# Attention and max-out layer on one core: operand splits moved in the time table, q and k loaded by halves, one ordered section instead of two, the last weight part on VectorE

## The chip, the cores and the metric

The kernel runs on one core of one Trainium2 chip. The metric is device time in microseconds of that core; the time before is the median of three runs. A profile of one further execution shows what each engine did. The engines are named as the profile names them: PE (TensorE matmul), PEld (TensorE weight load), DVE (VectorE), ACT (ScalarE), POOL (GpSimd) and SP (SyncE, which here only issues DMAs).

## The reference

Attention in chunks of 64 positions, then a layer that takes the largest of three products and multiplies it by an output matrix. Everything is float32.

```python
scores = scale * np.matmul(q_c, k_c.transpose(0, 1, 2, 4, 3))      # chunks of 64, head_dim 64
scores = scores - np.max(scores, axis=-1, keepdims=True)
attn = np.exp(scores)
attn = attn / (np.sum(attn, axis=-1, keepdims=True) + 1e-09)
out = np.matmul(attn, v_c)
...
x = np.ascontiguousarray(attn_out.transpose(0, 2, 1, 3)).reshape(B * S, H * D)   # 4608 x 512
h = np.maximum(np.maximum(x @ w1, x @ w2), x @ w3)                               # 512 -> 768
return (h @ w_out).astype(np.float32)                                            # 768 -> 512
```

## The kernel before

**Tiles and groups.** The 4608 tokens are 36 tiles of 128 tokens (two chunks with eight heads each). Four tiles make a group; there are nine groups, 0 to 8. A group's hidden products `x @ w` (lines 148 to 150, written into `pm`) need the `x` of all its four tiles, then its output products follow (same lines, from `hh`, `hl`, `woh`, `wol`). So that float32 accuracy comes out of fast products, every operand is split into a high part, rounded by ScalarE (`xh`, `hh`, `wh`, `woh`), and a low part, which is the operand minus its high part (`xl`, `hl`, `wl`, `wol`); each product is then three matmuls: low weight by high data (L148), high weight by low data (L149), high by high (L150).

**Attention of a tile** (`attention`, tiles 8 to 35). One DMA loads q and k of the tile together into `r` (1 MB). ScalarE casts q into `qs` (L270) and k in two halves into `kk` (L292); GpSimd subtracts to get the low parts (L274 for `qs`, L296 twice for `kk`). PE forms the scores `s` of chunk 0 and of chunk 1 (four matmuls each, L252); `s` is one PSUM buffer, so the second product waits until ScalarE (L258) and VectorE (L263) have taken the first out into `e`. VectorE takes the maximum, GpSimd subtracts it (L318), ScalarE exponentiates (L323), VectorE sums, GpSimd normalizes (L165), VectorE transposes into `et` (L338), ScalarE and VectorE split that into `ah` (L343, L347). `ah` goes through DRAM (`there`) and comes back as `aa` (L352, L359). `v` is loaded as `rv` and split into `vs` in the same way. PE forms `x` of both chunks from `aa` and `vs` (L252), ScalarE and VectorE take it out as `xs` (L258, L263), and `xh` (ScalarE, L373) and `xl` (VectorE, L378) are the tile's part of the next-but-one group's operand.

**What sets the order.** Each engine executes in the order in which the program hands it work. Two ordered sections are written: the first follows the list `FIRST` (weights, tiles 0 to 7, hidden layer of group 0); the second walks through the products of the remaining groups at a step of 0.6815 and takes every other operation from a heap when its due time has come. The due times are written in `attention` relative to the tile's first score product: `r` at -13.0, `qs` at -5.7 and -4.4, `kk` at -4.5, -3.9 and -2.0, -0.7, `xh` at 30.3, and so on. Between the two sections a scheduler has placed the first instructions of the second among the last of the first: the load of tile 8's `r` stands among the weight loads on SP, and its `qs` and `kk` splits stand ahead of the last weight parts on ScalarE and GpSimd. The token `Y65p` at the end of `FIRST` puts the low part of the last piece of the output weights (`wol`, L143) on GpSimd.

**A group's start.** The first L149 of a group's hidden products reads `xl` and waits for the `xl` of the group's last tile. That tile's `xh` and `xl` fall into the same stretch as the `qs` split of a later tile, on ScalarE one right behind the other.

Of the kernel before, what the change touches and what calls it, by code (L numbers as in the profile page):

```python
# [9 lines left out]
F32 = mybir.dt.float32  # L10
# [10 lines left out]
P = 128  # L21
# [6 lines left out]
PLAIN = 8  # L28
# [17 lines left out]
B51 F22f h30f C51 hh2f D51 X51 Y42 H51 W60 h31f B52 Y51 A52 hl2f C52 D52 h32f X52 B60 W61 A60 F30f C60 xh6 D60 H52  # L46
xl6 h40f at7 X60 Y52 W62 A61 F31f H60 Y60 V7 F32f C61 hh3f D61 h41f B61 hl3f A62 X61 B62 C62 W63 H61 D62 F40f h42f
X62 F41f W64 H62 Y61 Y62 A63 h50f F42f C63 hh4f D63 A64 hl4f B63 C64 h51f B64 X63 xh7 D64 W65 F50f X64 H63 H64 h52f
F51f Y63 Y64 B65 A65 F52f C65 hh5f D65 hl5f X65 xl7 H65 Y65p
"""  # L50


# [1 line left out]
def chunk_attn_maxout_kernel(  # L54
# [12 lines left out]
    nc = tc.nc  # L67
# [3 lines left out]
    att = ctx.enter_context(tc.tile_pool(name="att", bufs=1))  # L71
# [161 lines left out]

    halves_of = [slice(0, 64), slice(64, 128)]

    def attention(t, x_of, col):

# [1 line left out]
        st = {}  # L241
        ops = []

        def due(at, pe=0.0):
            return lambda fn: ops.append((at, pe, fn))
# [19 lines left out]
        def stack(at, low_at, name, tag, src):  # L265

            @due(at)
            def _():
                st[name] = att.tile([P, 2, 4, P], F32R, name=name, tag=tag, bufs=1)
                nc.scalar.copy(out=st[name], in_=src())  # L270

            @due(low_at)
            def _():
                nc.gpsimd.tensor_tensor(out=st[name][64:], in0=src()[64:], in1=st[name][64:].bitcast(F32), op=ALU.subtract)  # L274

        @due(-13.0)
        def _():
            st["r"] = att.tile([P, 2, 2, 4, P], F32, name="r", tag="raw", bufs=1)
            nc.sync.dma_start(out=st["r"], in_=qk2[t - PLAIN])

        @due(8.5)
        def _():
            st["rv"] = att.tile([P, 2, 4, P], F32, name="rv", tag="rv", bufs=1)
            nc.sync.dma_start(out=st["rv"], in_=v2[t - PLAIN])

        stack(-5.7, -4.4, "qs", "qs", lambda: st["r"][:, 0])
        for c in range(2):
            @due(-4.5 + 0.6 * c)
            def _(c=c):
                if c == 0:  # L290
                    st["kk"] = att.tile([P, 2, 4, 2, P], F32R, name="kk", tag="kk", bufs=1)
                nc.scalar.copy(out=st["kk"][:, c, :, 0, :], in_=st["r"][:, 1, c])  # L292

            @due(-2.0 + 1.3 * c)
            def _(c=c):
                nc.gpsimd.tensor_tensor(out=st["kk"][:, c, :, 1, :], in0=st["r"][:, 1, c],  # L296
                                        in1=st["kk"][:, c, :, 0, :].bitcast(F32), op=ALU.subtract)

        def e_of(c):
            if "e" not in st:  # L300
                st["e"] = ep.tile([P, 4, 2, 64], F32, name="e")
            return st["e"][:, :, c, :]

        for c in range(2):
            products((0.0, 3.3)[c], (1.0, 4.3)[c], ps_s, "s", lambda g, c=c: st["qs"][:, c, g, :],
                     lambda g, c=c: st["kk"][:, c, g].rearrange("p a x -> p (a x)"), lambda c=c: e_of(c))
# [57 lines left out]
        def x_cols(c):  # L364
            if "xs" not in st:
                st["xs"] = xs_p.tile([P, 4, P], F32, name="xs")
            return st["xs"][:, :, c * 64:(c + 1) * 64]

        for c in range(2):
            products((24.0, 27.7)[c], (25.0, 29.3)[c], ps_x, "x", lambda g, c=c: st["vs"][:, c, g, :],  # L370
                     lambda g, c=c: st["aa"][:, :, :, 2 * g + c].rearrange("p n a x -> p a n x"), lambda c=c: x_cols(c))
# [79 lines left out]
    starts = [sum(GROUPS[:i]) for i in range(len(GROUPS))]  # L451
    halves = {}
    def x_tiles(i):
        if i not in halves:
            halves[i] = [xp.tile([P, CT, 512], F32R, name=n) for n in ("xh", "xl")]
        return halves[i]
# [19 lines left out]
    def idle_products(n):  # L476
        ps = ps_m.tile([P, 512], F32, name="pm")
        for _ in range(n):
            nc.tensor.matmul(out=ps, lhsT=idle[:, :P], rhs=idle[:, :512], start=True, stop=True)

    nc.vector.memset(idle, 0.0)
    ET = mybir.EngineType
    with tc.manual_schedule(engines={ET.PE, ET.DVE, ET.Activation, ET.Pool, ET.SP}):
        for name in FIRST.split():
            if name[0] == "i":
                idle_products(int(name[1:]))
            elif name[-1] == "p":
                ops[name[:-1]](nc.gpsimd)
            elif name[:3] == "nrm":
                ops[name](nc.vector)  # L490
            else:
                ops[name]()
# [4 lines left out]
    due = []  # L497

    def plan(at, pe, fn):
        heapq.heappush(due, (at, len(order), pe, fn))  # L500
        order.append(fn)

    order = []
    for i in range(2, len(GROUPS)):
        for tt in range(4):
            first = (i - 1) * total - 33.0 + (tt - 3) * (15.4 if i == 2 else total / 4)
            for at, pe, fn in attention(starts[i] + tt, lambda i=i: x_tiles(i), tt * P):
                plan(first + at, pe, fn)

    parts = [g0["project"](0, 1), g0["project"](2), g0["project"](3)]  # L510
# [3 lines left out]
        parts += [g["project"](0, 1), g["project"](2), g["project"](3)]  # L514
    now = -4 * JT * STEP - 2 * BLOCK
    with tc.manual_schedule(engines={ET.PE, ET.DVE, ET.Activation, ET.Pool, ET.SP}):
        for part in parts:
            for after in part:
                now += STEP
                for at, fn in after:  # L520
                    plan(now + at, 0.0, fn)
                while due and due[0][0] <= now:
                    _, _, pe, fn = heapq.heappop(due)
                    fn()
                    now += pe
        while due:
            heapq.heappop(due)[3]()
# [42 lines left out]
```

## Time and profile before

| | before |
|---|---|
| median of 3 runs | 711.55 us (711.12 to 712.19) |
| the profiled execution: time, span | 709.78 us, 707.7 us |
| PE busy | 694.7 us (98%), 3401 instructions |
| DVE, ACT, POOL busy | 404.1, 356.3, 297.7 us (57%, 50%, 42%) |
| granted TensorE clock | 1.0 over the span |
| DMA | 121.20 MB, 171 GB/s in the mean |

A busy share near 100% says that PE has few idle moments, not that every one of its steps is as short as it can be. So the table of who waited for whom is read for PE, and then the timeline around each of these waits. In a row of the timeline the first number is the start in microseconds from the start of the span, the second the length (of all instructions of the row together, where x is more than 1), then follow engine, line, operation and tiles, and in brackets the idle time of the engine before it with what ended it.

### The profile page before, as it was taken

How to read it: one execution, taken by the hardware profiler on the slowest of the kernel's cores; microseconds unless marked ns; L12 is line 12 of the kernel's file. 1: busy time of each engine (PE TensorE's matmuls, PEld its weight loads, DVE VectorE, ACT ScalarE, POOL GpSimd, SP SyncE). 2: the span in 40 equal slices, each digit the busy share in tenths (PEclk: the TensorE clock that was granted, in tenths of full speed). 3: DMA queues.
4: the chain of work that ended last, by engine and by line, in shares of the span. 5: the costliest groups of instructions: out<-in, count | busy, mean ns of one | idle time of the engine just before them, and what ended most of it. 6: DMA issues, size and time to landing. Idle time of an engine off the chain costs nothing.

```text
span 707.7 us, 9475 instructions
## 1 busy us (share of the span) xinstructions
PE 694.7 (98%) x3401; PEld 575.6 (81%) x3402; DVE 404.1 (57%) x721; ACT 356.3 (50%) x663; POOL 297.7 (42%) x191
## 2 busy tenths in 40 slices
PE   8999999999999999999999999999999999999998
PEld 4998878778888888888888888888888888888886
DVE  6988863587466654665466546664666456622220
ACT  5666653556555554554555555555555545531111
POOL 1422033565545455555555555545445545510000
PEclk9999999999999999999999999999999999999999
DMA  9975414566755566555855385547555755440001
GB/s 359 370 282 179 144 38 171 169 193 196 223 176 178 164 210 192 179 179 145 271 178 157 113 265 157 167 149 241 163 167 178 223 170 173 119 134 15 1 1 59
DMA packets 38318, 121.20 MB, mean 171 GB/s; under 512 B 3456, under 2 KB 3456, under 8 KB 34688
## 3 DMA queue, kind: packets, MB, share of 16 engines
q1 hardware_dynamic: 38272, 120.60, 52.6%
q8 instruction: 27, 0.44, 0.3%
q14 instruction: 19, 0.16, 0.1%
HBM read 96.47 MB, written 24.12 MB: 170 GB/s over the span
## 4 chain that ended last, share of the span: by engine, by line
PE 72%; issue 7%; ACT 6%; POOL 6%; DVE 5%; DMA 4%; SPq 0%; POOLq 0%; ACTq 0%; DVEq 0%
PE pm L148 20%; PE pm L150 20%; PE pm L149 20%; PE s L252 4%; POOL kk L296 4%; PE x L252 4%; ACT qs L270 3%; DVE xs L263 2%; PE x L219 2%; DMA buf<-in_wout 2%; ACT xh L373 1%; PE s L186 1%; POOL qs L274 1%; DMA r<-in_qk 1%; DMA xl<-in_w 1%
## 5 line engine op out<-in xcount | busy, mean ns | idle before, releaser
L148 PE MATMUL pm<-xh,wl 128*128 128x512 f32 (+1 forms) x660 | 256.8, 389 | 0.0
L150 PE MATMUL pm<-xh,wh 128*128 128x512 f32 (+1 forms) x660 | 255.2, 387 | 0.0
L149 PE MATMUL pm<-xl,wh 128*128 128x512 f32 (+1 forms) x660 | 254.7, 386 | 0.0
L150 PEld LDWEIGHTS pm<-xh,wh 128*128 128x128 f32 x660 | 124.0, 188 | 26.4
L149 PEld LDWEIGHTS pm<-xl,wh 128*128 128x128 f32 x660 | 124.2, 188 | 22.3
L148 PEld LDWEIGHTS pm<-xh,wl 128*128 128x128 f32 x660 | 124.1, 188 | 22.0
L263 DVE TENSOR_TENSOR e<-s,e 64x256 f32<-64x256 f32 x112 | 47.3, 422 | 145.4 <-ACT e L258 144.6
L274 POOL TENSOR_TENSOR qs<-r,qs 64x1024 fp32r<-64x1024 f32 x28 | 70.5, 2517 | 110.0 <-ACT qs L270 83.5
L412 DVE TENSOR_TENSOR m<-pm,m 128x512 f32<-128x512 f32 (+1 forms) x110 | 74.7, 679 | 40.4 <-PE pm L150 38.5
L258 ACT COPY e<-s 64x256 f32<-64x256 f32 x112 | 41.2, 367 | 106.1 <-PE s L252 105.3
L149 PE MATMUL pm<-wol,hh 128*128 128x512 f32 x216 | 84.3, 390 | 0.8 <-POOL wol L143 0.8
L148 PE MATMUL pm<-woh,hl 128*128 128x512 f32 x216 | 84.7, 392 | 0.0
L150 PE MATMUL pm<-woh,hh 128*128 128x512 f32 x216 | 84.3, 390 | 0.0
L296 POOL TENSOR_TENSOR kk<-r,kk 128x512 fp32r<-128x512 f32 x56 | 79.3, 1436 | 2.2
L274 POOL TENSOR_TENSOR vs<-rv,vs 64x1024 fp32r<-64x1024 f32 x28 | 67.2, 2400 | 13.7 <-ACT vs L270 6.0
L258 ACT COPY xs<-x 64x256 f32<-64x256 f32 x112 | 41.1, 367 | 52.9 <-PE x L252 52.0
L421 DVE TENSOR_TENSOR hl<-m,hh 128x512 fp32r<-128x512 f32 (+1 forms) x54 | 56.0, 1036 | 19.1 <-ACT hh L418 18.6
L318 POOL TENSOR_TENSOR e<-e,mx 128x512 f32<-128x512 f32 x28 | 29.2, 1044 | 87.9 <-DVE mx L314 87.9
L165 POOL TENSOR_TENSOR e<-e,sm 128x512 f32<-128x512 f32 x31 | 32.4, 1044 | 73.0 <-DVE sm L162 72.6
L263 DVE TENSOR_TENSOR xs<-x,xs 64x256 f32<-64x256 f32 x112 | 47.3, 422 | 26.1 <-ACT xs L258 24.6
L418 ACT CAST hh<-m 128x512 fp32r<-128x512 f32 (+1 forms) x55 | 33.7, 613 | 48.5 <-DVE m L412 47.6
L410 ACT COPY m<-pm 128x512 f32<-128x512 f32 (+1 forms) x55 | 31.9, 580 | 37.0 <-DVE hl L421 21.2
(66 smaller groups left out, 785.3 us busy)
## 6 DMA issues: line engine op xcount, KB each, us to landing
r<-in_qk SPq DMA_DIRECT2D x28, 1024.0 KB, 6.0
aa<-there SPq DMA_DIRECT2D x56, 512.0 KB, 5.7
rv<-in_v SPq DMA_DIRECT2D x28, 512.0 KB, 5.4
there<-ah SPq DMA_DIRECT2D x28, 512.0 KB, 2.6
out_x<-ao SPq DMA_DIRECT2D x36, 256.0 KB, 2.2
buf<-in_qk SPq DMA_DIRECT2D x8, 768.0 KB, 8.4
buf<-in_w SPq DMA_DIRECT2D x10, 512.0 KB, 3.8
buf<-in_vb SPq DMA_DIRECT2D x8, 512.0 KB, 6.8
```

What stands on the lines that cost most here:

```text
L148: nc.tensor.matmul(out=o, lhsT=al, rhs=bh, start=first, stop=False)
L149: nc.tensor.matmul(out=o, lhsT=ah, rhs=bl, start=False, stop=False)
L150: nc.tensor.matmul(out=o, lhsT=ah, rhs=bh, start=False, stop=last)
L165: eng.tensor_tensor(out=e, in0=e, in1=sm.unsqueeze(2).broadcast_to([P, 8, 64]), op=ALU.mult)
L252: nc.tensor.matmul(out=o[:, g].rearrange("p a h x -> p (a h x)"), lhsT=lhs(g), rhs=rhs(g), start=True, stop=True)
L258: nc.scalar.copy(out=out()[rows], in_=st[name][rows, :, 0, h, :])
L263: nc.vector.tensor_tensor(out=out()[rows], in0=st[name][rows, :, 1, h, :], in1=out()[rows], op=ALU.add)
L274: nc.gpsimd.tensor_tensor(out=st[name][64:], in0=src()[64:], in1=st[name][64:].bitcast(F32), op=ALU.subtract)
L296: nc.gpsimd.tensor_tensor(out=st["kk"][:, c, :, 1, :], in0=st["r"][:, 1, c], in1=st["kk"][:, c, :, 0, :].bitcast(F32), op=ALU.subtract)
L412: nc.vector.tensor_tensor(out=banks[j][:, :n], in0=ps[j, w][:, :n], in1=banks[j][:, :n], op=ALU.max)
L418: nc.scalar.copy(out=hh[j][:, lo:hi], in_=banks[j][:, :hi - lo])
L421: eng.tensor_tensor(out=hl[j][:, lo:hi], in0=banks[j][:, :hi - lo], in1=hh[j][:, lo:hi].bitcast(F32), op=ALU.subtract)
```

## The change

Four edits. The `qs` and `kk` splits of a tile fall due earlier by `lead` (0.8 for the tiles of group 2, 1.5 for those of later groups). `r` is one buffer for all tiles, loaded by two DMAs of 0.5 MB, q due at -16.6 and k at -14.6. The list `FIRST` is worked off inside the same ordered section as the time table. The last token is `Y65`, which puts that low part on VectorE.

```diff
-F51f Y63 Y64 B65 A65 F52f C65 hh5f D65 hl5f X65 xl7 H65 Y65p
+F51f Y63 Y64 B65 A65 F52f C65 hh5f D65 hl5f X65 xl7 H65 Y65
...
-    def attention(t, x_of, col):
+    loaded = {}
+
+    def attention(t, x_of, col, lead):
...
-        @due(-13.0)
-        def _():
-            st["r"] = att.tile([P, 2, 2, 4, P], F32, name="r", tag="raw", bufs=1)
-            nc.sync.dma_start(out=st["r"], in_=qk2[t - PLAIN])
+        for half, at in enumerate((-16.6, -14.6)):
+            @due(at)
+            def _(half=half):
+                if "r" not in loaded:
+                    loaded["r"] = att.tile([P, 2, 2, 4, P], F32, name="r", tag="raw", bufs=1)
+                st["r"] = loaded["r"]
+                nc.sync.dma_start(out=st["r"][:, half], in_=qk2[t - PLAIN][:, half])
...
-        stack(-5.7, -4.4, "qs", "qs", lambda: st["r"][:, 0])
+        stack(-5.7 - lead, -4.4 - lead, "qs", "qs", lambda: st["r"][:, 0])
         for c in range(2):
-            @due(-4.5 + 0.6 * c)
+            @due(-4.5 + 0.6 * c - lead)
...
-            @due(-2.0 + 1.3 * c)
+            @due(-2.0 + 1.3 * c - lead)
...
-    with tc.manual_schedule(engines={ET.PE, ET.DVE, ET.Activation, ET.Pool, ET.SP}):
+    def first_group():
         for name in FIRST.split():
...
-            for at, pe, fn in attention(starts[i] + tt, lambda i=i: x_tiles(i), tt * P):
+            for at, pe, fn in attention(starts[i] + tt, lambda i=i: x_tiles(i), tt * P, 0.8 if i == 2 else 1.5):
...
     with tc.manual_schedule(engines={ET.PE, ET.DVE, ET.Activation, ET.Pool, ET.SP}):
+        first_group()
         for part in parts:
```

In the changed file the lines from `attention` on lie 3 to 9 lines further down (L270 becomes L273, L373 L380, L343 L350, L433 L440). PE executes the same instructions in the same order as before.

**ScalarE around the start of group 2.** `ao` is an output of group 1, `ah` and `xh` belong to older tiles, `qs` and `kk` are the splits of a later tile. Before:

```order
L433 COPY ao<-pm 128x512
L343 CAST ah<-et 128x2x256
L373 CAST xh<-xs 128x4x128
L270 CAST qs<-r 128x1024
L292 CAST kk<-r 128x4x128 x2
L433 COPY ao<-pm 128x512
```

Now:

```order
L440 COPY ao<-pm 128x512
L350 CAST ah<-et 128x2x256
L273 CAST qs<-r 128x1024
L380 CAST xh<-xs 128x4x128
L299 CAST kk<-r 128x4x128 x2
L440 COPY ao<-pm 128x512
```

`qs` has moved ahead of `xh`. The same exchange stands at every later tile that still has a `qs` split behind it, inside the groups as well as at the starts of groups 2 to 7; GpSimd and VectorE keep their order there.

**ScalarE at the end of the first group.** `woh` are the high parts of the output weights (the last one is piece 65), `buf` and `ao` prepare that piece, `qs` and `kk` belong to tile 8. Before:

```order
L140 CAST woh<-ao 128x512 x2
L270 CAST qs<-r 128x1024
L292 CAST kk<-r 128x4x128 x2
L124 ACTIVATE buf<-buf 128x512
L120 ACTIVATE ao<-buf 128x512
L418 CAST hh<-m 128x512
L140 CAST woh<-ao 128x512
```

Now:

```order
L140 CAST woh<-ao 128x512 x2
L124 ACTIVATE buf<-buf 128x512
L120 ACTIVATE ao<-buf 128x512
L425 CAST hh<-m 128x512
L140 CAST woh<-ao 128x512
L273 CAST qs<-r 128x1024
L299 CAST kk<-r 128x4x128 x2
```

Tile 8's splits now stand behind the last weight piece, on ScalarE and on GpSimd; `wol` of that piece has left GpSimd and stands on VectorE behind the last `xl` of the first group.

**SP around the first tiles of the time table.** `there` and `aa` carry `ah` through DRAM, `rv` is v. Before, tiles 8 and 9:

```order
L284 DMA rv<-in_v 128x1024
L352 DMA there<-ah 128x1024
L359 DMA aa<-there 64x4x512 x2
L279 DMA r<-in_qk 128x2048
```

Now:

```order
L291 DMA rv<-in_v 128x1024
L359 DMA there<-ah 128x1024
L286 DMA r<-in_qk 128x1024
L366 DMA aa<-there 64x4x512 x2
L286 DMA r<-in_qk 128x1024
```

The q half stands between `there` and `aa` at these two tiles; from tile 10 on both halves stand behind `aa`, where the whole load stood. The first load of `r` has moved from among the weight loads to behind the last of them.

## Rows read from the trace of the kernel before

**Rows 1.** Who waited for whom, PE alone: total us, times, longest

```profile
PE s L252 <- POOL kk L296: 4.5, 19, 1.1
```

**Rows 2.** Timeline, PE, around the two score products of a later tile

```profile
213.38 0.39 PE L150 MATMUL pm<-xh,wh 128*128 128x512 f32 x1
213.94 0.74 PE L252 MATMUL s<-kk,qs 128*128 128x256 f32 x4 [0.18 <-POOL kk L296]
214.52 0.40 PE L148 MATMUL pm<-xh,wl 128*128 128x512 f32 x1
...
217.02 0.39 PE L150 MATMUL pm<-xh,wh 128*128 128x512 f32 x1
217.25 0.64 PE L252 MATMUL s<-kk,qs 128*128 128x256 f32 x4
217.72 0.40 PE L148 MATMUL pm<-xh,wl 128*128 128x512 f32 x1
```

**Rows 3.** Timeline, other engines, ahead of that score product

```profile
207.03 0.62 ACT L343 CAST ah<-et 128x512 fp32r<-128x512 f32 x1 [1.38 <-DVE et L338]
207.92 0.62 ACT L373 CAST xh<-xs 128x512 fp32r<-128x512 f32 x1 [0.27 <-DVE xs L263]
208.45 1.04 ACT L270 CAST qs<-r 128x1024 fp32r<-128x1024 f32 x1
...
209.25 0.68 DVE L378 TENSOR_TENSOR xl<-xs,xh 128x512 fp32r<-128x512 f32 x1
...
209.62 2.57 POOL L274 TENSOR_TENSOR qs<-r,qs 64x1024 fp32r<-64x1024 f32 x1 [3.37 <-ACT qs L270]
...
209.85 0.68 DVE L412 TENSOR_TENSOR m<-pm,m 128x512 f32<-128x512 f32 x1
...
211.22 1.53 DVE L421 TENSOR_TENSOR hl<-m,hh 128x512 fp32r<-128x512 f32 x1 [0.69 <-ACT hh L418]
...
212.84 0.59 ACT L410 COPY m<-pm 128x512 f32<-128x512 f32 x1 [0.70 <-DVE hl L421]
```

**Rows 4.** Timeline, VectorE and GpSimd, where their subtractions overlap

```profile
153.81 2.40 POOL L274 TENSOR_TENSOR qs<-r,qs 64x1024 fp32r<-64x1024 f32 x1 [1.17 <-ACT qs L270]
154.75 2.01 DVE L347 TENSOR_TENSOR ah<-et,ah 128x512 fp32r<-128x512 f32 x1 [0.35 <-ACT ah L343]
156.29 3.32 POOL L296 TENSOR_TENSOR kk<-r,kk 128x512 fp32r<-128x512 f32 x2
156.69 1.77 DVE L421 TENSOR_TENSOR hl<-m,hh 128x512 fp32r<-128x512 f32 x1
```

**Rows 5.** Timeline around the start of a group's hidden products

```profile
262.91 0.62 ACT L343 CAST ah<-et 128x512 fp32r<-128x512 f32 x1 [0.21 <-DVE et L338]
...
264.45 0.69 DVE L378 TENSOR_TENSOR xl<-xs,xh 128x512 fp32r<-128x512 f32 x1
...
266.18 0.39 PE L149 MATMUL pm<-xl,wh 128*128 128x512 f32 x1
```

**Rows 6.** Copies of scores (the page's costliest groups), and a restart of PE

```profile
L258 ACT COPY e<-s 64x256 f32<-64x256 f32 x112 | 41.2, 367 | 106.1 <-PE s L252 105.3
...
160.62 0.86 DVE L263 TENSOR_TENSOR e<-s,e 64x256 f32<-64x256 f32 x2
161.63 0.71 PE L252 MATMUL s<-kk,qs 128*128 128x256 f32 x4 [0.20 <-ACT vs L270]
```

**Rows 7.** Timeline, the last piece of the output weights

```profile
101.67 0.62 ACT L140 CAST woh<-ao 128x512 fp32r<-128x512 f32 x1 [4.19 <-DVE ao L137]
103.69 0.50 PE L149 MATMUL pm<-wol,hh 128*128 128x512 f32 x1 [0.84 <-POOL wol L143]
```

**Rows 8.** Timeline, PE, two waits at tiles 10 and 9

```profile
141.21 0.74 PE L252 MATMUL s<-kk,qs 128*128 128x256 f32 x4 [1.12 <-POOL kk L296]
150.33 0.73 PE L252 MATMUL x<-aa,vs 128*128 128x256 f32 x4 [0.36 <-DMA aa<-there]
```

**Rows 9.** DMA issues (the page): KB each, median us to landing

```profile
r<-in_qk SPq DMA_DIRECT2D x28, 1024.0 KB, 6.0
```

## The prediction

> **What bounds the kernel now.** I read the table of who waited for whom for PE first, then the timeline around each wait. PE is busy 98% of the span, so only its waits and what could become one matter. The table has one repeated wait: the score products wait for `kk` from GpSimd, 19 times, 4.5 us idle in all [rows 1]. One of these is 1.12 us [rows 8]; the other 18 are 0.19 us each. I count 17 of them from 213.94 on, at three of four tiles, and one at tile 11.
>
> What one costs is more than its idle time. From the matmul before the scores to the matmul behind them PE takes 1.14 us with the wait (213.38 to 214.52) and 0.70 us without (217.02 to 217.72) [rows 2]. So a wait costs its idle time plus 0.26 us, here 0.44 us; 0.11 us of it is lost behind the restart (0.58 against 0.47 us from the scores to the next matmul). The chain behind it: ScalarE does `ah`, `xh`, `qs`; GpSimd starts its `qs` 1.17 us after ScalarE's, having idled 3.37 us, and `kk` follows [rows 3].
>
> **The lock that decides this case.** A VectorE subtraction of two SBUF tiles that starts while GpSimd is in one of its subtractions ends only 0.55 us after GpSimd's end: `ah` asked at 154.75, GpSimd's `qs` ended at 156.21, `ah` at 156.76 [rows 4]; `hl` asked at 211.22, `qs` ended at 212.19, `hl` at 212.75 [rows 3]. Alone such a subtraction takes 0.68 us. It works the other way too: `qs` takes 2.57 us where `xl` had started before it [rows 3], 2.40 us else [rows 4]. `m`, which reads PSUM, is not held: 0.68 us in the middle of `qs` [rows 3].
>
> **Part 1, `qs` ahead of `xh`: the gain.** ScalarE starts an operation 0.09 us before the one before it ends (`xh` ends at 208.54, `qs` starts at 208.45 [rows 3]). So the `qs` cast now starts at 207.03 + 0.62 - 0.09 = 207.56 instead of 208.45, and GpSimd's `qs` 1.17 us later, at 208.73 instead of 209.62. It ends at 211.13, and the first `kk`, even with the delay of part 3, at 212.83; PE wants it at 213.38. The wait goes: 17 x 0.44 = **7.5 us gained**.
>
> **Part 2, the same exchange at a group's start: the loss.** `xh` now starts 0.95 us behind the `qs` cast and `xl` 0.03 us behind the end of `xh`; before, `xl` asked ahead of GpSimd's `qs`, now behind it. At the start of a group [rows 5]: `ah` 262.91, `qs` cast 263.44, GpSimd's `qs` 264.61 to 267.01, `xh` 264.39 to 265.01, `xl` asks at 265.04, is held, and ends at 267.56 instead of 265.14. PE's first L149 stands at 266.18 [rows 5] and needs it. PE restarts 0.15 us after VectorE's end (160.62 + 0.86 = 161.48, restart at 161.63 [rows 6]), so at 267.71: 1.53 late, plus 0.11 behind the restart, 1.64 us. Until now these starts had no wait; `xl` ended 1.0 us ahead. Groups 2 to 7 have a `qs` split there, group 8 has none: 6 x 1.64 = **9.8 us lost**. Bounds: 0 if `xl` still gets in first, 9.8 if not; I take 9.8, because 0.43 us (264.61 to 265.04) separate the two requests.
>
> **Part 3, the exchange inside a group.** There nobody waits for `xl`, but VectorE is in order behind it. `xl` asks at 209.25 and ends at 211.13 + 0.55 = 211.68 instead of 209.93. The first `kk` takes 1.15 us from the release: of the pair in [rows 4] the first ended 0.55 us before the end of `hl` (158.46), at 157.91, `ah` having ended at 156.76. So it ends at 212.83, and the second one starts. `m` starts 0.08 us before the end of `xl`, at 211.60, and `hl` asks 1.37 us after that (209.85 to 211.22 [rows 3]), at 212.97: 0.14 us after the second `kk`, which I give 1.25 us (1.15 after a release, a little more from its own start). `hl` is held until 214.08 + 0.55 = 214.63. ScalarE's `m` waits for `hl` (0.09 us: 212.75 to 212.84 [rows 3]) and starts at 214.72; behind it stand the two copies of the first scores, from 215.22 to 215.95 (0.367 us each [rows 6]); VectorE's half takes 0.86 us [rows 6], to 216.83; PE restarts at 216.98. Without a wait the second score product would start at 217.25 - 0.44 = 216.81 [rows 2]. Loss 0.17 + 0.11 = 0.28 us. This needs `hl` and `m` of the next block in that place, which two tiles of each of six groups have; at the other two ScalarE copies outputs there. 12 x 0.28 = **3.4 us lost**, bounds 0 and 5.3 (12 x 0.44, as long as the wait it replaces).
>
> **Part 4, the last weight part.** PE waited 0.84 us for `wol` [rows 7], so 1.10 us. On VectorE it costs 0.68 us instead of waiting for GpSimd. Were `woh` no earlier (102.29 [rows 7]), `wol` would end at 103.0, still 0.4 us past PE's 102.59, and half the gain would stay. But `woh` idled 4.19 us for VectorE [rows 7], which tile 8's `kk` held by the lock; those now stand behind it. I take the whole: **1.1 us gained** (bounds 0.5 and 1.1). Tile 8's own splits come later, at latest 102.2 + 1.17 + 2.40 + 1.25 = 107.0. Its scores had no wait; I price this at nothing, and if the cover is gone at no more than tile 10's wait, 1.4 us.
>
> **Part 5, tiles 9 to 11.** Tile 10's wait (1.12 + 0.26 = 1.38 us) goes by part 1, but the time is waited for at 150.33, where `x` of tile 9 waits for `aa` [rows 8]: its chain starts from `ah`, which nothing here makes earlier. By the lock `ah` comes later by up to one `kk`, 1.25 us; I take 0.75. Tile 11's waits, 0.44 and 0.46 us (161.63 [rows 6]), go. Sum 0.75 - 0.90 = -0.15, so **0.2 us gained**, bounds 2.3 gained and 0.4 lost.
>
> **Part 6, loads and section.** 28 more DMA issues lie on SP, which waits most of the time. From tile 10 on the halves stand where the whole stood, and each waits for fewer readers. At nothing; the two q halves ahead of `aa` are a rival below.
>
> **Sum.** -7.5 + 9.8 + 3.4 - 1.1 - 0.2 = +4.4 us. On the profiled execution (span 707.7, 709.78 with what lies around it) this gives 714.2; it lay 1.8 us under the median of the runs, to which the forecast goes: 711.55 + 4.4 = **716.0 us**.
>
> **Two rules beside it.** The 0.14 us of part 3 have no row of their own: no two requests of the trace lie so close. The Trainium skill, "SBUF — State Buffer", section "Who interferes with whom", says that whichever issues first gets the shared port pair for its whole instruction; by that the second `kk` keeps it and the sum stands. Against it, "Perfetto Trace Analysis", section "GPSIMD Engine Instruction", has a GpSimd span in a profile as unreliable; by that 0.14 us are undecided and 712.6 would be as likely. The steady 0.55 us in the rows speak for usable ends, so I lean to the first.
>
> **Rivals.**
> - *`hl` gets in ahead of the second `kk`.* The condition is 0.14 us. Then part 3 costs nothing, 716.0 - 3.4 = 712.6, and `ah` of tile 9 wins the same race, worth up to 1 us more: 711.6 to 712.6. Chance 0.14.
> - *The start of a group does not wait: faster.* If GpSimd's `qs` starts 0.43 us later than worked out there, `xl` goes first, ends before 266, and parts 1, 4 and 5 remain: 711.55 - 8.8 = 702.7, with part 3 706.1. For it speaks that 0.43 us rest on three added offsets, against it that all three are read from rows. Chance 0.13.
> - *The q halves delay `aa`: slower still.* At tiles 8 and 9 a 0.5 MB load now goes out ahead of `aa`. 1 MB takes 6.0 us to land [rows 9], so up to 3.0 us, and `x` of tile 9 has no slack: up to 719.0. Against it: `aa` is issued only when `there` has landed, and the load can use that gap. Chance 0.07.
>
> **How the numbers follow.** The forecast, 716.0, has 0.66; its own range is 714 to 718 from the bounds of parts 3 to 5. The range 710.5 to 718.5 takes in the first rival and leaves out the second and the end of the third. Below 0.2% (1.4 us, 710.1 to 713.0), about what a measurement of this kernel can tell from no change, lie the first rival and a little of the forecast's edge: same 0.15, faster 0.13, slower 0.72.
>
> **What would show it.** Right: PE waits for `xl` at six group starts, about 1.4 us idle each; the score waits on `kk` from 213 on are gone; second score products start 0.2 us late at twelve tiles; `xl` inside a group takes about 2.4 us instead of 0.68; `wol` no longer ends a wait. Wrong: `xl` of 0.68 us at the group starts (second rival), or `hl` that ends before the second `kk` starts (first).

## The result and the profile after

The changed kernel takes 715.1 us (median of 7 runs, 713.0 to 717.3), the kernel before 711.5 us on the same chip. The ratio is 1.0048, with a 95% interval of 1.0026 to 1.0071: slower, as forecast (716.0 us, range 710.5 to 718.5). The profiled execution of the changed kernel took 712.97 us with a span of 711.1 us, against 709.78 us and 707.7 us before. PE is busy 98% of the span in both.

The table of who waited for whom, PE alone (total us, times, longest), has changed its rows. The wait for `kk` of [rows 1] is gone; in its place stands one that did not exist:

```profile
PE pm L149 <- DVE xl L385: 7.6, 6, 1.3
PE x L255 <- DMA aa<-there: 1.7, 1, 1.7
...
PE s L255 <- DVE e L266: 1.1, 2, 0.8
```

The timeline around the start of group 3's hidden products, which answers to [rows 5] (start, length, engine, line, operation and tiles, idle before with its cause):

```profile
261.83 1.05 ACT L273 CAST qs<-r 128x1024 fp32r<-128x1024 f32 x1
262.78 0.61 ACT L380 CAST xh<-xs 128x512 fp32r<-128x512 f32 x1
...
263.43 2.52 DVE L385 TENSOR_TENSOR xl<-xs,xh 128x512 fp32r<-128x512 f32 x1 [0.54 <-ACT xh L380]
...
263.01 2.39 POOL L277 TENSOR_TENSOR qs<-r,qs 64x1024 fp32r<-64x1024 f32 x1 [2.48 <-ACT qs L273]
...
264.34 0.39 PE L148 MATMUL pm<-xh,wl 128*128 128x512 f32 x1
266.01 0.50 PE L149 MATMUL pm<-xl,wh 128*128 128x512 f32 x1 [1.27 <-DVE xl L385]
```

The reader is to see the order on three engines. ScalarE's `qs` cast stands ahead of `xh`, GpSimd's `qs` starts 0.42 us ahead of `xl`, and `xl`, which took 0.69 us in [rows 5], takes 2.52 us: it ends at 265.95, 0.55 us after GpSimd's 265.40. PE has nothing else to do and restarts at 266.01. Before, at the same place, `xl` asked at 264.45 [rows 5] and GpSimd's `qs` started a full microsecond later:

```profile
265.50 2.40 POOL L274 TENSOR_TENSOR qs<-r,qs 64x1024 fp32r<-64x1024 f32 x1 [3.37 <-ACT qs L270]
```

Inside a group, the same tile as in [rows 3]:

```profile
207.70 0.61 ACT L380 CAST xh<-xs 128x512 fp32r<-128x512 f32 x1
...
213.92 0.59 ACT L417 COPY m<-pm 128x512 f32<-128x512 f32 x1 [0.84 <-DVE hl L428]
214.41 0.75 ACT L261 COPY e<-s 64x256 f32<-64x256 f32 x2
...
208.44 2.44 DVE L385 TENSOR_TENSOR xl<-xs,xh 128x512 fp32r<-128x512 f32 x1
...
212.16 1.67 DVE L428 TENSOR_TENSOR hl<-m,hh 128x512 fp32r<-128x512 f32 x1 [0.69 <-ACT hh L425]
...
207.93 2.40 POOL L277 TENSOR_TENSOR qs<-r,qs 64x1024 fp32r<-64x1024 f32 x1 [2.49 <-ACT qs L273]
210.40 2.88 POOL L303 TENSOR_TENSOR kk<-r,kk 128x512 fp32r<-128x512 f32 x2
```

The two `kk` of the last row are 210.40 to 212.03 and 211.98 to 213.28. `hl` asks at 212.16, so after the first and inside the second, and ends at 213.83, again 0.55 us after GpSimd. ScalarE's `m` waits 0.84 us for it, with the two score copies behind it.

To split the difference I compared the start of every score and `x` product in the two traces, in the same order, since PE executes the same list. Behind the last group start the changed kernel is 3.10 us late. The steps of this shift, in us: -1.09 by 95 us (the start, below), -1.35 where PE waited for `wol`, +0.08 over tiles 9 to 11, +1.55 to +1.61 at each of six group starts (9.47 together), -0.17 to -0.24 at eleven tiles and +0.07 at a twelfth near 461 us (-2.10 together), -0.43 to -0.47 at each of five (-2.23), and +0.32 near 482 us, whose cause stays open.

### The profile page after: what moved, and what is told of

Its sections match the earlier page's. It is cut to its first block, busy times and chain, and to the rows that moved or that the text cites. A ratio compares the mean times of both kernels' runs of the same rounds, so it can differ in the third digit from the quotient of the medians.

```text
span 711.1 us, 9546 instructions
## 1 busy us (share of the span) xinstructions
PE 694.0 (98%) x3401; PEld 575.7 (81%) x3402; DVE 446.1 (63%) x722; ACT 353.8 (50%) x663; POOL 300.5 (42%) x190
## 4 chain that ended last, share of the span: by engine, by line
PE 90%; DVE 5%; DMA 2%; issue 1%; ACT 1%; POOL 0%; SPq 0%; ACTq 0%; POOLq 0%
PE pm L149 26%; PE pm L148 26%; PE pm L150 26%; PE s L255 4%; PE x L255 4%; DVE xl L385 2%; PE x L219 2%; PE s L186 1%; DMA aa<-there 1%; PE tp L208 1%; DMA xh<-in_w 0%; DVE hl L428 0%; DMA there<-ah 0%; DVE ao L137 0%; DVE ah L354 0%
## 5 line engine op out<-in xcount | busy, mean ns | idle before, releaser
L149 PE MATMUL pm<-xl,wh 128*128 128x512 f32 (+1 forms) x660 | 255.4, 387 | 7.6 <-DVE xl L385 7.6
L149 PEld LDWEIGHTS pm<-xl,wh 128*128 128x128 f32 x660 | 124.2, 188 | 32.2 <-DVE xl L385 10.1
L277 POOL TENSOR_TENSOR qs<-r,qs 64x1024 fp32r<-64x1024 f32 x28 | 67.1, 2396 | 92.3 <-ACT qs L273 92.1
L149 PE MATMUL pm<-wol,hh 128*128 128x512 f32 x216 | 84.2, 390 | 0.0
L303 POOL TENSOR_TENSOR kk<-r,kk 128x512 fp32r<-128x512 f32 x56 | 80.8, 1465 | 2.2
L277 POOL TENSOR_TENSOR vs<-rv,vs 64x1024 fp32r<-64x1024 f32 x28 | 73.1, 2610 | 16.4 <-issue 8.5
L428 DVE TENSOR_TENSOR hl<-m,hh 128x512 fp32r<-128x512 f32 (+1 forms) x54 | 57.9, 1072 | 19.2 <-ACT hh L425 18.6
L385 DVE TENSOR_TENSOR xl<-xs,xh 128x512 fp32r<-128x512 f32 x28 | 60.9, 2174 | 4.6 <-ACT xh L380 4.6
```

The lines of the kernel that those rows point to most:

```text
L149: nc.tensor.matmul(out=o, lhsT=ah, rhs=bl, start=False, stop=False)
L385: nc.vector.tensor_tensor(out=xl[:, :, col:col + P], in0=st["xs"], in1=xh[:, :, col:col + P].bitcast(F32), op=ALU.subtract)
L428: eng.tensor_tensor(out=hl[j][:, lo:hi], in0=banks[j][:, :hi - lo], in1=hh[j][:, lo:hi].bitcast(F32), op=ALU.subtract)
```

## The experiments

All times are medians; a ratio is to the kernel before, run on the same chip. The kernel before took 710.8, 710.6 and 711.6 us in the three sessions below.

### The exchange of the splits, place by place

Four kernels differ in `lead` alone, or have it alone. **start_kept** takes the old due times back, from group 3 on, at the one tile of each group that falls on the next group's start:

```diff
-... tt * P, 0.8 if i == 2 else 1.5):
+... tt * P, 0.8 if i == 2 else 0.0 if tt == 1 else 1.5):
```

> The changed kernel with one edit: at the second tile of each group, the one whose splits stand where the next group starts, the splits of q and k go back to their old due times; everywhere else they stay 1.5 earlier. Theory A (the loss lies in the six group starts, where the low part xl is held until GpSimd's qs has ended): the six waits of 1.27 us, each with its restart 1.54 us, go, the score waits on kk inside the group stay away, and the second score products at 12 tiles still start 0.27 us late: 715.1 - 6 x 1.54 = 705.9 us. Rival B (the halves of q and k, or the one ordered section, cost the time; the group starts only take over waiting that would come anyway): at least 713 us. Rival C (the time is lost inside the group, because VectorE's xl and hl are held there and everything behind comes later): about 715 less 1 to 2 us.

Measured: 705.9 us, ratio 0.9935 (0.9922 to 0.9948). The waits of L149 are gone. At the same group start as above, `xl` is in and out before GpSimd's `qs` begins:

```profile
261.60 0.62 ACT L380 CAST xh<-xs 128x512 fp32r<-128x512 f32 x1 [0.27 <-DVE xs L266]
262.12 1.05 ACT L273 CAST qs<-r 128x1024 fp32r<-128x1024 f32 x1
...
262.25 0.69 DVE L385 TENSOR_TENSOR xl<-xs,xh 128x512 fp32r<-128x512 f32 x1
...
263.30 2.40 POOL L277 TENSOR_TENSOR qs<-r,qs 64x1024 fp32r<-64x1024 f32 x1 [3.37 <-ACT qs L273]
```

**start_only** does the opposite, the exchange at that tile alone:

```diff
-... tt * P, 0.8 if i == 2 else 1.5):
+... tt * P, 1.5 if i > 2 and tt == 1 else 0.0):
```

> The changed kernel with the opposite edit: the splits of q and k are 1.5 earlier only at the second tile of each group from group 3 on, the one at the next group's start; everywhere else they stand at their old due times. Theory A: the score waits inside the group return (17 waits, 7.5 us), the 12 late second score products go (12 x 0.27 = 3.2 us), the group starts wait as in the changed kernel: 715.1 + 7.5 - 3.2 = 719.4 us, with 5 or 6 waits of L149 for xl of 1.3 us in the trace. Rival B (halves or section): as the kernel with no exchange, 713 or more, with no larger step than that. Rival C (the loss is inside the group): 711 or less.

Measured: 718.5 us, ratio 1.0105 (1.0089 to 1.0121). It has both waits in its table:

```profile
PE pm L149 <- DVE xl L385: 7.6, 6, 1.3
PE s L255 <- POOL kk L303: 4.5, 18, 1.1
```

**no_lead** has no exchange at all (`lead` 0.0 everywhere):

> The changed kernel with the splits at their old due times everywhere: what remains of the change is q and k by halves of one buffer, the one ordered section, and the last weight part on VectorE. Theory A: as the kernel before without the wait for wol, 711.5 - 1.35 = 710.2 us; the 17 score waits on kk are back, no wait of L149 for xl. Rival B (the halves or the section cost the time): 714 or more.

Measured: 709.85 us, ratio 0.9989 (0.9978 to 1.0000). Up to the first score product of the time table it is 1.18 us ahead of the kernel before; some of that is given back where `x` waits for `aa`, 0.97 us at tile 9 and 0.53 us at 500 us.

What follows: the two kernels that differ only in the exchange at the group starts differ by 8.7 us (718.5 - 709.85) without the others and, by the ratios, by 8.0 us with them ((1.0048 - 0.9935) x 711.5). In the traces start_only falls behind no_lead by 1.55 to 1.57 us at each of the six starts. Halves, section and `wol` together do not make the kernel slower; rivals B and C of these expectations fall.

**lead_alone** puts the earlier due times into the kernel before and nothing else (the diff is that of `stack` and `kk` in the change, with the 0.8 and 1.5).

> The kernel before with the earlier due times of the splits of q and k alone (0.8 earlier in group 3, 1.5 from group 4 on): q and k still whole, two sections, the last weight part on GpSimd. Theory A: the six group starts wait for xl as in the changed kernel, the score waits on kk inside the group go, and the wait for wol of 0.84 us stays: 715.1 + 1.35 = 716.5 us. Rival B (the halves or the section cost the time): 711.5 or less.

Measured: 721.8 us, ratio 1.0147 (1.0120 to 1.0174), 5.3 us more than I had worked out. Neither theory has it. Its trace shows a wait of ScalarE for a load, in the group of the `qs` cast in the view by lines (after the bar busy us, mean ns, idle us before):

```profile
L270 ACT CAST qs<-r 128x1024 fp32r<-128x1024 f32 x28 | 29.4, 1049 | 7.3 <-DMA r<-in_qk 7.3
```

One such wait in its timeline, and PE's wait behind it, since ScalarE's copies of `x` stand behind that cast:

```profile
134.49 1.05 ACT L270 CAST qs<-r 128x1024 fp32r<-128x1024 f32 x1 [2.67 <-DMA r<-in_qk]
...
137.85 0.71 PE L252 MATMUL x<-aa,vs 128*128 128x256 f32 x4 [2.27 <-DVE xs L263]
```

So a new theory: the earlier splits need the halves. **lead_halves** is lead_alone with the two loads of the change:

```diff
-        @due(-13.0)
-        def _():
-            st["r"] = att.tile([P, 2, 2, 4, P], F32, name="r", tag="raw", bufs=1)
-            nc.sync.dma_start(out=st["r"], in_=qk2[t - PLAIN])
+        for half, at in enumerate((-16.6, -14.6)):
+            @due(at)
...
+                nc.sync.dma_start(out=st["r"][:, half], in_=qk2[t - PLAIN][:, half])
```

> The kernel before with two parts of the change: the earlier splits and the halves of q and k (two sections and the last weight part on GpSimd stay). With the earlier splits alone and q and k whole it took 721.8 us, 5.3 more than worked out, and its trace has the cast of q waiting 7.3 us for the load r. Theory D (the earlier splits need the halves: a cast that is due earlier waits for the whole 1 MB, with ScalarE's hh and the copies of x behind it): the casts wait for no load, 715.1 + 1.35 (the wait for wol) = 716.5 us. Rival (the 5.3 us come from the two sections or from the granted clock): 720 or more.

Measured: 714.75 us, ratio 1.0060 (1.0043 to 1.0077), 7.0 us less than lead_alone, 6.2 us by the ratios. No cast of `qs` waits for a load any more:

```profile
L272 ACT CAST qs<-r 128x1024 fp32r<-128x1024 f32 x28 | 29.3, 1045 | 0.0
```

The halves show no gain by themselves (no_lead) and some 6 us together with the exchange. Not all of that is waiting for loads. In the two profiled executions lead_alone falls 3.7 us behind lead_halves up to tile 11, where two of its casts wait 2.67 and 2.98 us for their load, and 3.0 us at the first group start, behind a third such wait of 1.28 us. Some 1.6 of these 3.0 us are eight products that ran at a lower granted clock, told at the end. The three runs of lead_alone with a granted clock of 0.997 took 721.2 to 723.2 us, the one with 1.0 took 718.0 us.

### What holds `xl`, and what delays the second score product

**qs_low_written_only** keeps every order and replaces one GpSimd operation per tile; the low part of q is left out of the computation.

```diff
-                nc.gpsimd.tensor_tensor(out=st[name][64:], in0=src()[64:], in1=st[name][64:].bitcast(F32), op=ALU.subtract)
+                if name == "qs":
+                    nc.gpsimd.memset(st[name][64:].bitcast(F32), 0.0)
+                else:
+                    nc.gpsimd.tensor_tensor(...)
```

> The changed kernel with the order of its splits kept everywhere, but GpSimd's difference for the low part of q replaced by a fill with zeros (the low part of q is left out of the computation, nothing else): an operation that reads no buffer and holds VectorE no longer than it runs. Theory A (xl at the group start is held by that difference): xl takes 0.7 us as before, the six waits of L149 go, 715.1 - 9.3 = 705.8 us, and somewhat less if hl also gets away (down to 702.5). Rival (the wait comes from ScalarE: xh ends 1 us later behind the qs cast, whatever GpSimd does): the six waits stay, 714 to 715 us. Rival (any work of GpSimd holds VectorE's subtraction, a fill too): xl waits for the end of the fill, and the loss shrinks with the fill's length only.

Measured: 702.2 us, ratio 0.9881 (0.9862 to 0.9901). At a group start the fill runs where the subtraction ran, `xh` is as late as in the changed kernel, and `xl` passes while the fill is still going; PE's first L149 of `xl` waits for nothing:

```profile
188.71 0.62 ACT L383 CAST xh<-xs 128x512 fp32r<-128x512 f32 x1
...
188.92 0.95 POOL L278 MEMSET qs<- 64x1024 f32 x1 [2.46 <-issue]
...
189.36 0.69 DVE L388 TENSOR_TENSOR xl<-xs,xh 128x512 fp32r<-128x512 f32 x1 [0.55 <-ACT xh L383]
...
190.53 0.39 PE L149 MATMUL pm<-xl,wh 128*128 128x512 f32 x1
```

So it is not the later `xh`, and not any work of GpSimd, but the subtraction that holds `xl`. The six group starts come 1.55 to 1.61 us earlier against the changed kernel; the twelve second score products also come some 0.25 us earlier (`hl` asks at 210.37 instead of 212.16 at the tile shown of after, whose first scores stand 0.03 us apart in the two traces, and is out in time, though a `kk` still holds it). With both gone, 702.2 us is the lower end of what was expected.

**start_kept_two_m** gives `m` a second buffer, in start_kept:

```diff
-    mp = ctx.enter_context(tc.tile_pool(name="mp", bufs=1))
+    mp = ctx.enter_context(tc.tile_pool(name="mp", bufs=2))
```

> The kernel with the old order at the group starts alone, and a second buffer for m, the running maximum of the mixture's block. Theory A (the second score product is 0.27 us late at 12 tiles because ScalarE's next m waits for hl, which is held until GpSimd's second kk has ended, and the two score copies stand behind that m): m finds a free buffer, the copies run at once, the 12 delays go: 705.9 - 12 x 0.27 = 702.7 us. Rival (the delay comes from VectorE, whose share of the score sums stands behind the held hl): the copies come early but the sum does not, 705.9 us.

Measured: 704.0 us, ratio 0.9905 (0.9881 to 0.9929); a second time 705.4 us, 0.9913 (0.9898 to 0.9929). The mechanism holds: `hl` is held as before, but ScalarE's `m` and the score copies no longer stand behind it.

```profile
212.48 0.59 ACT L417 COPY m<-pm 128x512 f32<-128x512 f32 x1
212.96 0.75 ACT L261 COPY e<-s 64x256 f32<-64x256 f32 x2
...
211.53 1.68 DVE L428 TENSOR_TENSOR hl<-m,hh 128x512 fp32r<-128x512 f32 x1 [0.69 <-ACT hh L425]
```

Against start_kept all twelve second score products come earlier, eleven by 0.17 to 0.20 us plus 0.06 to 0.08 us behind the restart and one by 0.54 us. That is 3.3 us. In the trace 1.86 us remain at the end: 0.24 us was there at the start, and some 1.7 us were lost again at five products of `x` (0.2 us at tile 9, then 0.36, 0.16, 0.58 and 0.31 us near 293, 349, 478 and 497 us), mostly in longer waits for `aa`. By the ratios the gain is 2.1 us in one session and 1.6 us in the other, with intervals that overlap that of start_kept, so the size of what is left stays open.

### Where the waits for `aa` come from

In the kernels with halves PE waited 1.5 to 4.2 us for `aa`, before 0.4 us [rows 8]. First guess: q's half, which goes out 1.3 us behind `aa`, slows it. **start_kept_two_m_k_first** loads k's half first, from group 3 on, which a release of `kk` holds back:

```diff
-        for half, at in enumerate((-16.6, -14.6)):
+        for half, at in ((0, -16.6), (1, -14.6)) if t < 12 else ((1, -16.6), (0, -14.6)):
```

> The kernel with the old order at the group starts and two buffers of m, with k's half loaded ahead of q's half from group 3 on. In the kernels with halves the load of q goes out 1.3 us behind the two loads aa, ahead of it before it went out 3 to 8 us behind, and PE waits for aa 1.5 to 2.7 us in all instead of 0.4. Theory E (q's half shares the way with aa and delays it): k's half is released only by the last kk of the tile before, so both halves go out later, aa lands in 5.7 us at the median as in the kernel before, its waits from group 3 on go (about 1.2 us in the trace of the kernel without two buffers): 702.7 - 1 = 701.7 us. Rival (the landing of aa varies by itself): 702.7 us, waits for aa as often as before.

Measured: 705.4 us, ratio 0.9917 (0.9896 to 0.9937), no gain. Mostly the halves go out some 3 us behind `aa` now, and the waits stay:

```profile
PE x L255 <- DMA aa<-there: 4.1, 5, 1.5
```

The guess fell. Following one late `aa` back, not its own landing is late but that of `there`, from which it reads. The DMA view of start_kept_two_m from 280 to 287 us (queue, packets, MB, share of 16 engines; then loads with KB and us to landing):

```profile
q8 instruction: 1, 0.02, 0.9%
...
aa<-there SPq DMA_DIRECT2D x2, 512.0 KB, 5.9
there<-ah SPq DMA_DIRECT2D x1, 512.0 KB, 4.4
```

`aa` lands in 5.9 us, as everywhere; `there` takes 4.4 us, where it mostly takes 2.6. In the same stretch lies one packet of the queue q8, instructions. That queue carries 27 packets in a run, and PE has 6804 instructions, one packet for about 252 of them if the packets are PE's. So I moved the packets against the work, by more and smaller idle products ahead of the first load, in start_kept_two_m:

```diff
-        for _ in range(n):
-            nc.tensor.matmul(out=ps, lhsT=idle[:, :P], rhs=idle[:, :512], start=True, stop=True)
+        for cols in [512] * 7 + [256] * 40 if n == 27 else [512] * n:
+            nc.tensor.matmul(out=ps[:, :cols], lhsT=idle[:, :P], rhs=idle[:, :cols], start=True, stop=True)
```

> The same kernel with 20 of the 27 idle products at PE's start cut in two (40 products of 256 columns instead of 20 of 512): the same columns and results, 40 PE instructions more (20 products, 20 weight loads) ahead of everything. Theory F (a packet of the instruction queue q8, 27 of them for 6804 instructions of PE, so one for about 252, delays the load there if it falls into it): the packets come 40 instructions, some 4 us, earlier in PE's work; counted along the trace none of the 19 packets between 128 and 611 us then lies in a there. The three late landings go, and with them the waits of x for aa from group 3 on (1.19, 0.58 and 0.41 us, 0.3 more with their restarts): 704.0 - 2.4 = 701.6 us. Rival G (there is late at these places for another reason, and the packet only stands beside it): late landings and waits at the same places, 704.0 us.

**fetch_132** has `[512] * 5 + [128] * 88` in that place:

> The same kernel with 22 of the 27 idle products cut in four (88 products of 128 columns): 132 PE instructions more ahead of everything. Theory F: the packets come 132 instructions, some 13 us, earlier, and by the count along the trace 11 of the 19 then fall into a there (near 171, 190, 246, 302, 394, 412, 431, 486, 505, 560 and 597 us), whose landings take 3 to 4.7 us, while those near 281, 337 and 467 take 2.6: more waits of x for aa than five, and a time of 705 to 708 us. Rival G: the late landings stay near 281, 337 and 467, 704.0 us.

**start_kept_two_m_again** ran beside them:

> The kernel with the old order at the group starts and two buffers of m once more, unchanged, on the same chip as the next two: 704.0 us (its first run: 703.99, single runs 701.5 to 707.5). Its trace should show the same three late landings of there (near 281, 337 and 467 us, 3.7 to 4.7 us instead of 2.6), each with one packet of the instruction queue q8 inside it, and the waits of x for aa behind them.

Measured: 705.4 us (0.9913, 0.9898 to 0.9929) without a move, 702.6 us (0.9880, 0.9866 to 0.9893) with 40 instructions, 702.0 us (0.9869, 0.9851 to 0.9887) with 132. In fetch_40 the DMA view from 280 to 287 us has no row of q8 any more, and the load is on time:

```profile
there<-ah SPq DMA_DIRECT2D x1, 512.0 KB, 2.6
```

Its one wait for `aa` past 150 us, 1.39 us at 550, stands behind a `there` at 538 into which a packet now falls (view from 538 to 541):

```profile
q8 instruction: 1, 0.02, 3.0%
...
there<-ah SPq DMA_DIRECT2D x1, 512.0 KB, 4.7
```

Theory F holds in part. In both kernels no packet falls into the loads near 281, 337 and 467 us any more, and all six are on time, 2.60 to 2.63 us. But a packet inside the load is not enough to make it late. Of the five that fell into a `there` past 128 us in the two kernels, two made it late (4.67 us at 538 in fetch_40, 3.65 us at 373 in fetch_132), and the other three loads took 2.70 to 2.86 us. The count along the trace was poor too: for fetch_40 it promised no packet in a `there` past 128 us and there were two, for fetch_132 eleven and there were three, so that kernel, foreseen as the slowest, is the fastest of all. Packets do not move by a constant number of PE's instructions.

The medians, 2.9 and 3.4 us below start_kept_two_m_again, seem to overstate what the loads are worth: two of its six runs had a granted clock of 0.995 and took 706.4 and 706.8 us. In the profiled executions, from the first score product of the time table on, the gains are 1.1 and 2.3 us, and PE's waits for `aa` fall from 3.7 us to 3.0 and 1.6 us.

## Why the prediction was right

**Part 2, the group start, carries it.** Forecast 1.64 us at each of six starts, 9.8 in all; the traces show 1.55 to 1.61, 9.5 in all, with 1.27 us of wait each. The request of `xl` came 0.42 us behind GpSimd's `qs` (0.43 worked out), and the end 0.55 us behind GpSimd's. PE restarted 0.06 us after `xl`, not the 0.15 us taken from a restart behind another row. start_kept, start_only and qs_low_written_only show it three ways: the exchange taken away there alone, made there alone, and the holder replaced with all orders kept. The second rival (no wait at the start, 702.7 to 706.1 us) is what start_kept is made into, at 705.9 us.

**Part 1, the gain inside the group.** The 17 waits went. One is worth 0.45 us in the five tiles without part 3 (0.34 at the first product, 0.11 behind the restart), against 0.44 forecast.

**Part 3, the chain over `xl`, `m` and `hl`.** Forecast 0.28 us at twelve tiles, 3.4 in all. Against the 0.45 us that five tiles without it gain, eleven of the twelve lose 0.21 to 0.28 us and the one near 461 us loses 0.52 us, 3.3 in all. The 0.14 us on which the first rival rested came out as the spans of the trace say: `hl` asks at 212.16, 0.13 us after the end of the first `kk`, and waits for the second. The first rival fell. The doubt about GpSimd's spans (the Trainium skill, "Perfetto Trace Analysis", section "GPSIMD Engine Instruction") was not needed. The ends lie 0.55 us apart in every pair shown here, and 0.54 to 0.56 us in all 505 pairs counted below. A fill of GpSimd let `xl` pass in 0.69 us, a subtraction made it 2.44 to 2.52 us. The Trainium skill, "SBUF — State Buffer", section "Who interferes with whom", says just this: a VectorE instruction with two SBUF inputs contends with a GpSimd instruction that reads SBUF, not with one that only writes it. The trace agrees.

**Part 4, `wol`.** Forecast 1.1 us, measured 1.35: I left out that behind the restart PE also loses time, as at the scores.

**Part 5, tiles 9 to 11.** Forecast 0.2 us gained, measured 0.08 lost. Its mechanism was right: `x` of tile 9 waits 1.69 us for `aa`, because its chain starts from `ah`. That is held by GpSimd's second `kk` and ended 1.69 us earlier than before, where PE ahead of it had gained 2.44: 0.75 us lost, the amount taken, which was a guess between 0 and 1.25. The next step, `there`, took 2.86 us instead of 2.63, which makes 0.99 us. Tile 11 gave 0.91 us back (0.90 forecast). The forecast missed a wait at tile 10's second score product, for VectorE's `e`, which adds nothing here, since `x` of tile 9, behind it, has to wait for `aa` anyway:

```profile
141.71 0.71 PE L255 MATMUL s<-kk,qs 128*128 128x256 f32 x4 [0.84 <-DVE e L266]
...
148.88 0.71 PE L255 MATMUL x<-aa,vs 128*128 128x256 f32 x4 [1.69 <-DMA aa<-there]
```

**Part 6, loads and section, "at nothing".** True of the sum: no_lead, which has them without the exchange, is not slower than the kernel before. But I priced the halves beside the exchange and not as its condition. Whole loads would, by lead_alone, have made the changed kernel some 6 us slower still, part of it by the clock, since a cast that comes 1.5 earlier meets a load that has not landed. The third rival (the q halves that go out ahead of `aa` at tiles 8 and 9) did cost something, but 0.2 us and not up to 3.0: in all eleven kernels with halves `there` takes 2.8 to 3.0 us at these two tiles, and 2.6 us with whole loads (before and lead_alone). The two `aa` of tile 9 took 5.02 and 6.79 us, before 4.99 and 6.71. The longer waits for `aa` at later tiles are another matter, told above.

**The sum.** 4.4 us forecast; 3.10 us in the two traces, 3.4 us by the ratio (0.0048 x 711.5). The parts as measured add up to 4.2 us, more than 3.10, by the start: the profiled run of after began its first scores 0.75 us earlier (9.04 against 9.79) and was 1.09 us ahead at 95 us, which no part of the change explains. no_lead, with the same first group, began at 9.95:

```profile
9.95 2.00 PE L186 MATMUL s<-buf 128*128 128x64 f32 x16 [1.08 <-DMA buf<-in_qk]
```

In the eleven other traces of changed kernels the first scores begin at 9.66 to 10.33, so after alone is early, and I count that as scatter.

**A kernel faster than both** came out of it: the exchange inside the groups, not at their starts (705.9 us), with a second `m` and the packets moved, 702.0 us, ratio 0.9869.

## What to carry to other kernels

When two engines hold each other in one kind of instruction, the order in which they ask decides more than their lengths: before moving work earlier, list at every place what it now gets ahead of, and price the places apart, since here the same exchange gained 0.17 to 0.47 us at 16 of 17 places inside a group and lost 1.55 to 1.61 us at its start. An edit that is worth nothing alone can be the condition of another; try it both with and without. And where one wait comes back at the same few microseconds of every run, look into the DMA view of that stretch for a queue that is not the kernel's own.

## What the runs showed of the hardware that I had not expected

**How steady the hold of a VectorE subtraction is.** Over the 13 traces 505 subtractions of VectorE with both inputs in SBUF (`ah`, `hl`, `xl`) asked while GpSimd was in a subtraction and took more than 0.9 us, up to 2.52. Every one of them ended 0.54 to 0.56 us after that of GpSimd. The only ten that took less had asked within the last 0.35 us of GpSimd's. `m`, which reads PSUM, asked 461 times when GpSimd's instruction had more than 0.4 us to go and never took more than 0.69 us, and neither did the 23 `xl` that asked as early in a fill.

**Instruction loads can delay data loads.** Over the 13 traces of this case there are 364 loads of `there` (0.5 MB). In 36 of them a packet of q8 lies between issue and the issue of `aa`, and 31 of these took 3.0 to 4.7 us; of 317 with no instruction packet 6 did, and the median is 2.6 us; in three of these 6 a packet of q8 that had started up to 0.8 us ahead of the load was still under way. All but five of the 36 are the same three loads of the other eleven kernels, so the experiment with moved packets says more than the count. Of eleven with a packet of q14 alone nine took 3.0 to 3.6 us. Why some packets delay a load and others do not was not tried.

**In one trace the granted clock fell in mid-run, behind a wait of 2 us at a group start.** In lead_alone the first group start waited 0.31 us for `xh` and then 2.02 us for `xl`. Within 1.5 us of the restart the granted clock fell to 0.50, that is from 2.4 to 1.2 GHz, and came back some 3.5 us later (columns: stretch, length, PE busy, instructions, granted clock, DMA share, GB/s):

```profile
198.00:199.00 1.00, 1.00 (x5) 0.77 0.60 121
199.00:200.00 1.00, 1.00 (x4) 0.50 1.13 313
200.00:201.00 1.00, 1.00 (x4) 0.50 1.02 205
201.00:202.00 1.00, 1.00 (x4) 0.53 1.10 246
202.00:203.00 1.00, 1.00 (x6) 1.00 1.26 258
```

A matmul of 512 columns took 0.63 instead of 0.39 us there, and the shift at this start was 4.50 us instead of 1.56 at the next. The mean granted clock of the run was 0.997. This is one case; whether the wait was the cause is open. The single runs of the changed kernel show, without a trace, that time and granted clock go together: 716.1 to 717.3 us at 0.996 and 0.997, 713.0 to 715.1 us at 0.999 and 1.0. In its profiled run the clock did not fall, so where it falls in the others stays open.
